# A two-branch attention kernel: shared PSUM banks, paired queries, adding DMAs and a shift pass on GpSimd

## The chip, the cores and the metric

The kernel runs on one core of one Trainium2 chip. The metric is the device time of one execution, in microseconds. The engines are named as in the profile: PE (TensorE, matmuls), DVE (VectorE), ACT (ScalarE), POOL (GpSimd), SP (SyncE, which issues the DMAs here). PSUM, where the PE writes, has eight banks of 128 x 512 fp32.

## The reference

x has 2048 rows of 512. Branch A is full attention with 32 heads of 16; branch B is attention over eight earlier rows at distances 0, 2, ... 14 of the same x, with its own weights. A gate per row mixes them.

```
scores = einsum("bhqd,bhkd->bhqk", q, k) * (Dh ** -0.5)      # A: 32 heads, 2048 x 2048
o = einsum("bhqk,bhkd->bhqd", softmax(scores), v);  a = o @ A_wo
logits = einsum("bhsd,bhswd->bhsw", q, kg) * scale            # B: kg, vg = k, v at s - 2w, w = 0..7
o = einsum("bhsw,bhswd->bhsd", softmax(where(mask, logits, -1e9)), vg);  b = o @ B_wo
g = sigmoid((x * gate_w).sum(-1));  out = g * a + (1 - g) * b
```

## The kernel before, in words

**Branch A.** The queries are cut into four blocks of 512 (QW) and the heads into eight groups of four (NG). A *period* is one block and one group: 32 periods. In a period each of 16 key tiles of 128 meets four heads: 64 score blocks of 128 keys x 512 queries. The PE makes them (`qk`) in *sets* of three and two blocks, which go to two rings of PSUM banks (rA three, rB two). ACT turns a set into exp(scores), the bf16 tile pT (`ex`), three buffers a ring. The PE multiplies pT by V with a column of ones, so that acc, one bank, holds numerator and denominator of four heads (`pv_run`, `pv_mm`). At the end of a period DVE transposes acc to accT (`po1`), inverts the denominators (`po2`), POOL multiplies by the gate and the inverse (`po2a`, `po2b`), DVE transposes into oat (`po3`), and after eight periods the output products follow.

**339 blocks beside ACT.** `n_dve` (line 20) gives 3 to 12 blocks a period, 339 of 2048 in all, to DVE (`d_set`). The PE writes such a score into the bank D (`dq`), and DVE makes from it, with one multiply and add in integers, a number whose bits are roughly those of the exponential (`p1`, into a dt buffer). Three blocks make a group. For each group three shift passes (`sh`) add a constant to the 1536 integers, into pd buffers, and the PE adds all NV = 4 versions into acc with V weighted by WEIGHTS (vd_all), which smooths the error of the rough exponential.

**Queries.** `q_proj` makes Q for one period: 16 matmuls with 32 columns each, because four heads have to lie on rows 32 j and each is stored twice, plain and as absolute value (wq2). DVE copies the result out (`ev`, 0.68 us) and masks the sign bits of the second half (`ab`).

**Branch B.** For each of 16 row tiles (`b_tile`) the PE makes k, v and q; k and v go to DRAM (kv_scr), and SP loads them back shifted, in two halves of four distances (ksh, vsh, 512 KB each). POOL does nearly all the arithmetic in pieces of 128 x 256: products, tree of additions, softmax, the products with v (`av_mul`) and 14 additions of them (`av_add`), into obb. The PE transposes obb (`fin`) for the output products.

**PSUM.** rA 3, rB 2, misc 1, acc 1, D 1. misc is the one bank of all projections of both branches, their evictions and the zero matmuls that keep the PE busy.

**The order.** All work is written down as operations with an engine, planned duration, due time (`dl`), what they depend on, and buffers that they take and use (`Op`, `tok`). `list_schedule` (line 159) plays them out with these durations, each engine taking the candidate that is due first among those that can start soon. The order that comes out is the program's: each engine works its own list in that order, and waits in place if something is late. `avail` asks when a buffer of a resource comes free, `start` gives a due time its bonuses, GFIRST puts POOL's short steps ahead, URG raises work that holds misc. A buffer resource is a count (`Res`), and its buffers go round in turn.

Of the kernel before, what the change touches and what calls it, by code (L numbers as in the profile page):

```python
# [9 lines left out]
ALU = mybir.AluOpType  # L10
# [10 lines left out]
    dve_tiles=3,  # L21
# [15 lines left out]
DEXP = 56  # L37
NV = 4
NGR = 3
NPD = 3  # L40
# [4 lines left out]
NDE = 2  # L45
NDL = 4
SPREAD = (0.75, 0.8)
STEP = 32.0
WEIGHTS = (0.240234375, 0.2021484375, 0.169921875, 0.142578125)
# [10 lines left out]

class Tok:
    def __init__(self, res):
        self.res, self.ops = res, []


class Op:

    def __init__(self, eng, occ, fn, dl, deps=(), alloc=(), use=(), lat=None, rel=0.0, name="",
                 mode="f", js=(), full=0.0, fill=False, scores=None, after=(), ride=False, parts=None):
        self.scores, self.ride, self.parts = scores, ride, parts  # L70
# [17 lines left out]
GFIRST = -300.0  # L88
PRE = 0.14
GP = lambda kind, n: [(False, PRE), (True, NS[kind] * n)]  # L90
# [11 lines left out]
P1D, SHD, LASTD, PO1D = -100.0, 2.0, 200.0, 300.0  # L102
# [56 lines left out]
def list_schedule(ops, zeros):  # L159
# [15 lines left out]

    def avail(o):
        t = o.ready
        for tk in o.alloc:
            r = tk.res
            n = len(r.order)  # L180
            if n >= r.cap:
                for u in r.order[n - r.cap].ops:
                    if u.done is None:
                        return INF
                    t = max(t, u.end + SELF[u.eng] if u.eng == o.eng else u.done)
        return t

    arr = Array()

    def start(e, o):  # L190
        t = avail(o)
        if t == INF:
            return t, 0.0
        if e != "pe":
            return max(free[e], t), o.dl
        t0, end, _, _ = arr.plan(o, t)
        rides = o.mode == "r" and arr.mode == "r" and end < arr.end + 0.05
        return t0, o.dl + ((ALONE if o.ride else KEEP) if o.mode != arr.mode else 0.0) - (RIDE if rides else 0.0)
# [3 lines left out]
    while len(out) < len(ops):  # L202
# [24 lines left out]
        if e == "pe":  # L227
            tz, n = arr.idle(o, t)
            if n > 0:
                z = zeros(n)  # L230
                tz = max([tz, avail(z)] + [u.t for tk in z.alloc[0].res.order[-2:] for u in tk.ops if u.done is not None and u.t < t])
                if tz + n * PASS + (0.0 if o.mode == "c" else SWITCH) <= t + 0.05:
                    for tk in z.alloc:
                        tk.res.order.append(tk)
# [3 lines left out]
        for tk in o.alloc:  # L238
            tk.res.order.append(tk)
# [16 lines left out]
        out.append(o)  # L256
        for s_ in succ.get(o, ()):
            left[s_] -= 1
            if left[s_] == 0:
                s_.ready = max([s_.rel] + [d.end + SELF[d.eng] if d.eng == s_.eng else d.done for d in s_.deps] + [d.t for d in s_.after])  # L260
                cand[s_.eng].append(s_)
# [4 lines left out]
def kernel(  # L266
# [29 lines left out]

    def misc_ps(shape, dtype=FP32, tag="misc"):
        return ps.tile(shape, dtype, tag=tag, bufs=1, name="misc_ps")
# [50 lines left out]
    def op(eng, occ, fn, dl, **kw):  # L349
        if any(tk.res is res.get("misc") for tk in kw.get("use", ())):  # L350
            dl -= URG[eng]
# [6 lines left out]
    def tok(tag, cap):  # L358
        if tag not in res:
            res[tag] = Res(cap)  # L360
        return Tok(res[tag])
# [30 lines left out]
    for pi, (own, groups) in enumerate(seq):  # L392
        n = sum(len(g) for g in groups)
        left = [(gi, u_) for gi, g in enumerate(groups) for u_ in g]
        total, taken = len(own), 0
        for t, j in own:
# [4 lines left out]
            if left and n - len(left) < n * taken / (SPREAD[n // 10] * total) and all(u_[0] == pi for u_ in cur):  # L401
                js = [u_[2] for u_ in cur]
                pick = [x for x in left if x[0] == left[0][0] and x[1][1] not in js]
                if not pick and n - len(left) + 1 < n * taken / (SPREAD[n // 10] * total):
# [12 lines left out]
    wq2 = const.tile([128, DC, H, 2, DH], BF16, name="wq2")  # L417
# [6 lines left out]
    NH = NG // 2  # L424
    woarr = const.tile([128, NH, D], BF16, name="woarr")
    ident = const.tile([128, 128], BF16, name="ident")
    identf = const.tile([128, 128], FP32, name="identf")
    rowc = const.tile([128, 3], FP32, name="rowc")
    wts = const.tile([128, NV], BF16, name="wts")
# [7 lines left out]
    vd_all = const.tile([128, NV, NTD, H, DH + 1], BF16, name="vd_all")  # L437
# [5 lines left out]
    pd_a = const.tile([128, NPD * NGR * ROW], BF16, name="pd_a")  # L443
# [3 lines left out]
    pd_bufs = [pd_a[:, k_ * NGR * ROW:(k_ + 1) * NGR * ROW].rearrange("p (q n) -> p q n", q=NGR) for k_ in range(NPD)]  # L447
    stage = [pd_a[:, k_ * DC * D:(k_ + 1) * DC * D].rearrange("p (c n) -> p c n", c=DC) for k_ in range(2)]
    ott2 = const.tile([128, 2, BPC, 32], BF16, name="ott2")
# [3 lines left out]
    e1 = const.tile([128, NT], FP32, name="e1")  # L453
    d1 = const.tile([128, NT], FP32, name="d1")

    def init_dve():
# [9 lines left out]
        for m in range(NV):  # L466
            V.memset(wts[:, m:m + 1], WEIGHTS[m] * 2.0 ** -DEXP)

# [10 lines left out]
    def init_pool2():  # L479
        make_identity(nc, identf[:])  # L480
# [19 lines left out]
    def load_x(sc):  # L500
        def s():
            xl = work.tile([128, W // 2, D], BF16, name="xld", tag="gat", bufs=NGA) if sc < NGA else stage[1]
# [4 lines left out]
    wst = {}  # L507

    def load_w(part):
        def s():  # L510
            if part == 0:
                wst["q"] = stage[0]
                out = wst["q"]
            else:
                out = wkv[:, :, (part - 1) * D:part * D]
# [18 lines left out]
    tw = tok("pd", NPD)  # L534
# [7 lines left out]
    o_wq = op("sp", 0.5, load_w(0), -8.5, lat=12.5, alloc=[tw])  # L542
# [13 lines left out]
    def q2(E, i):  # L556
        def s():
            a0 = wst["q"][:, :, 4 * i * DH:4 * (i + 1) * DH]
# [6 lines left out]
    o_q2 = [op("dve", 0.5, q2(V, 0), 0.0, deps=[o_wq], use=[tw])]  # L565
    o_q2 += [op("pool", 1.5, q2(G, i), 4.0 + i, deps=[o_wq, o_k3[1]], use=[tw]) for i in range(1, NG)]
# [5 lines left out]
    o_warm = op("pe", 4.0, warm, -9.0, deps=[o_init_d], alloc=[tok("misc", 1)])  # L572
# [34 lines left out]
    def k_proj(i, sc, tag, dl, rel=0.0):  # L607
        st = {}
        tk = tok(tag, 1)
# [16 lines left out]
    def k_bound(i, dl):  # L626
        st = {}
        tk = tok("acc" if i == 0 else "misc", 1)
# [741 lines left out]
```

## Time and profile before

| | us |
|---|---|
| median of 3 runs | 826.01 (825.94 to 826.19) |
| profiled execution, time | 826.04 |
| profiled execution, span of the core | 824.3 |
| first pT starts | 19.67 |
| last pT ends | 815.49 |
| last POOL piece of branch B ends | 796.50 |

The span runs from the first to the last instruction; granted clock 0.994. A group of the profile is a set of instructions with the same tiles: their number, busy time together, mean duration in ns, and the idle time of the engine before them with what ended it. Nearly all instructions are recorded at a helper's line (L323, L332), so tiles tell them apart: pT<-ring is the exponential, acc<-pT the product with V, misc_ps<-bw a projection of branch B, dt_a<-D and wkv<-D the rough exponential (wkv serves as dt buffers once the K and V weights are used up), pd_a<-dt_a and pd_a<-wkv a shift pass. Rows that the steps use:

| row | count | mean ns |
|---|---|---|
| DVE shift pass pd_a<-dt_a, pd_a<-wkv | 195 + 144 | 941, 945 |
| DVE rough exponential | 195 + 144 | 680, 682 |
| DVE eviction of Q, mask | 32, 32 | 684, 538 |
| POOL products prod<-vsh,lg | 256 | 652 |
| POOL additions ob<-prod, ob<-ob,prod, obb<-ob,prod | 32, 64, 32 | 726, 729, 732 |
| POOL copies wq (256 bf16), wk (448 bf16) | 14, 2 | 400, 562 |
| PE Q projections misc_ps<-xT,wq | 512 | 382 (overlapping) |

SP's DMAs: ksh and vsh 512 KB in 3.9 and 3.7 us from issue to landing, kvs 256 KB in 2.0, out 128 KB in 1.7.

### The profile page before, as it was taken

The numbers are of one execution on the slowest core, as the hardware profiler recorded it, in microseconds if no ns is written. First come the engines' busy times: TensorE is split into PE (matmuls) and PEld (weight loads), VectorE is DVE, ScalarE is ACT, GpSimd is POOL, SyncE is SP. The second block draws the span as 40 slices with busy tenths as digits, with TensorE's granted clock in tenths as the row PEclk, the third lists the DMA queues.
The fourth block names the chain that finished last, engine by engine and source line by source line (L and its number), as shares of the span: only waits on it lengthen the run. The fifth ranks groups of instructions, "written<-read, shape, count | busy, mean of one in ns | idle before, by whom it ended". The sixth has DMA issues, their size and how long they took to land.

```text
span 824.3 us, 18657 instructions
## 1 busy us (share of the span) xinstructions
PE 777.9 (94%) x7314; PEld 247.4 (30%) x7358; DVE 706.3 (86%) x1111; ACT 785.9 (95%) x706; POOL 720.4 (87%) x1196
## 2 busy tenths in 40 slices
PE   7999999999999999999999999999999999999996
PEld 4333433333322222222222222222222222222231
DVE  5456876788978999989999899999989899998987
ACT  3899999999899899999999999999999999999995
POOL 5097999999999999899999999899999999899960
PEclk9899999999999999999999999999999999999999
DMA  9203020112111220211112111211111211110000
GB/s 296 78 3 116 2 90 28 65 52 65 57 48 65 65 66 28 63 53 47 63 35 77 57 50 51 65 53 49 43 52 54 82 34 65 52 52 27 27 1 26
DMA packets 44440, 47.37 MB, mean 57 GB/s; under 512 B 2352, under 2 KB 41776, under 8 KB 44352
## 3 DMA queue, kind: packets, MB, share of 16 engines
q1 hardware_dynamic: 44352, 46.18, 17.6%
q8 instruction: 57, 0.93, 0.5%
q14 instruction: 31, 0.25, 0.1%
HBM read 39.85 MB, written 6.32 MB: 56 GB/s over the span
## 4 chain that ended last, share of the span: by engine, by line
ACT 47%; PE 31%; issue 18%; DVE 2%; DMA 1%; SPq 0%; DVEq 0%; ACTq 0%
ACT pT L323 46%; PE acc L332 11%; PE ring L332 9%; PE misc_ps L332 8%; PE D L332 3%; DMA xld<-in_A_x_dram 1%; ACT lg L323 1%; DVE pd_a L323 0%; DVE kt_all L323 0%; PE pxt L584 0%; PE misc_ps L1011 0%; DVE dt_a L323 0%; DVE qt L323 0%; DVE vp_all L323 0%; DVE wkv L323 0%
## 5 line engine op out<-in xcount | busy, mean ns | idle before, releaser
L323 ACT ACTIVATE pT<-ring 128x1536 bf16<-128x1536 f32 (+1 forms) x684 | 778.8, 1319 | 20.5 <-PE acc L332 14.0
L332 PE MATMUL ring<-qt,kt_all 32*128 32x512 bf16 x1709 | 272.0, 382 | 28.4 <-ACT pT L323 19.2
L323 POOL TENSOR_TENSOR prod<-prod 128x256 f32<-128x256 f32 x352 | 235.6, 677 | 13.2
L332 PE MATMUL acc<-pT,vp_all 128*17 128x512 bf16 (+1 forms) x1709 | 189.0, 385 | 0.3 <-DVE accT L323 0.2
L323 POOL TENSOR_TENSOR prod<-ksh,qb 128x256 f32<-128x256 bf16 x256 | 166.5, 673 | 22.5 <-DMA ksh<-kv_scr 21.7
L323 DVE TENSOR_SCALAR pd_a<-dt_a 128x1536 uint16<-128x1536 uint16 x195 | 180.4, 941 | 1.2
L332 PEld LDWEIGHTS <-kt_all 32*128 32x128 bf16 x2048 | 91.2, 91 | 294.1 <-issue 285.2
L323 DVE TENSOR_SCALAR dt_a<-D 128x512 uint16<-128x512 f32 x195 | 132.7, 680 | 39.2 <-PE D L332 38.5
L323 POOL TENSOR_TENSOR prod<-vsh,lg 128x256 f32<-128x256 bf16 x256 | 162.0, 652 | 0.0
L323 DVE TENSOR_SCALAR pd_a<-wkv 128x1536 uint16<-128x1536 uint16 x144 | 131.0, 945 | 1.9 <-PE acc L332 0.3
L332 PE MATMUL acc<-pd_a,vd_all 128*17 128x512 bf16 x1017 | 130.0, 381 | 0.0
L332 PE MATMUL D<-qt,kt_all 32*128 32x512 bf16 x339 | 128.7, 380 | 1.0 <-DVE kt_all L323 0.4
L323 DVE TENSOR_SCALAR wkv<-D 128x512 uint16<-128x512 f32 x144 | 98.2, 682 | 7.5 <-PE D L332 5.9
L332 PE MATMUL misc_ps<-z 128*32 128x512 bf16 x260 | 85.3, 387 | 1.6 <-DVE z L323 1.6
L332 PEld LDWEIGHTS <-vp_all 128*17 128x17 bf16 (+1 forms) x1709 | 43.7, 88 | 74.9 <-issue 66.6
L332 PEld LDWEIGHTS <-vd_all 128*17 128x17 bf16 x1356 | 42.3, 88 | 64.3 <-issue 51.5
L332 PE MATMUL misc_ps<-bw,xT 128*128 128x512 bf16 x162 | 51.6, 393 | 2.4 <-DVE kt_all L323 0.8
L323 POOL TENSOR_TENSOR ob<-ob,prod 128x256 f32<-128x256 f32 x64 | 45.5, 729 | 0.0
L332 PEld LDWEIGHTS <-z 128*32 128x32 bf16 x341 | 29.9, 96 | 42.2 <-issue 26.1
L332 PEld LDWEIGHTS <-xT 128*128 128x128 bf16 x576 | 30.2, 98 | 36.8 <-issue 31.8
L332 PE MATMUL misc_ps<-xT,wq 128*32 128x512 bf16 x512 | 40.5, 382 | 0.1
L323 DVE TENSOR_SCALAR_CACHE_REDUCE kt_all<-misc_ps,rowc 128x512 bf16<-128x512 f32 x32 | 23.8, 746 | 16.0 <-PE misc_ps L332 15.4
(85 smaller groups left out, 611.9 us busy)
## 6 DMA issues: line engine op xcount, KB each, us to landing
ksh<-kv_scr SPq DMA_DIRECT2D x32, 512.0 KB, 3.9
vsh<-kv_scr SPq DMA_DIRECT2D x32, 512.0 KB, 3.7
kv_scr<-kvs SPq DMA_DIRECT2D x16, 256.0 KB, 2.0
out_dram<-osb SPq DMA_DIRECT2D x16, 128.0 KB, 1.7
xld<-in_A_x_dram SPq DMA_DIRECT2D x3, 512.0 KB, 6.4
bw<-in_B_wqkv_dram SPq DMA_DIRECT2D x1, 1536.0 KB, 11.5
wkv<-in_A_wqkv_dram SPq DMA_DIRECT2D x2, 512.0 KB, 7.3
pd_a<-in_A_x_dram SPq DMA_DIRECT2D x1, 512.0 KB, 8.4
```

The costliest lines, as they stand in the source:

```text
L323: return chain_on(key, f(*a, **k))
L332: return chain(nc.tensor.matmul(out, lhsT=lhsT, rhs=rhs, start=start, stop=stop, **kw))
```

## The change

It has seven parts, made together.

1. **Three shared banks.** misc, acc and D are replaced by three banks that any of them may take; which one is settled by the list, at each taking. At most two acc are open at once (`acc_two`).
2. **Queries by eight heads.** Periods 0 and 1 keep `q_proj`. From then on one product of 128 columns makes Q of two periods (`q_pair`); DVE copies it out once and masks it once, and SP writes both to DRAM (q_scr) and reads them back in the layout of each period: two writes and two reads a pair. qt has four buffers, not three.
3. **Adding DMAs.** The products with v of the first half go to av (four slots), those of the second half to prod; POOL issues a DMA that adds prod to av in place, twice, and a third that adds two slots of av to the other two. One addition in two pieces remains. The last two tiles keep additions on POOL. prod has three buffers.
4. **A list with margins.** What another engine awaits from POOL is planned 3 to 4 us later than it should be there (MARGIN). Products with V get a bonus when ACT is four sets ahead (PVU, PVN).
5. **One shift pass a period on POOL**, the third pass of a period's first group (POOL_G), with a buffer of its own.
6. The unshifted version of the rough exponential uses V itself, the others use weights relative to it (DEXP, WEIGHTS, three copies in vd_all, of four tiles now). `dq` waits for the dt buffer and for vd_all, where `p1` did.
7. Buffers: dt one early and three late, for two and four; accT, ott2, oat, obt one each, for two. The rough exponentials of a period are spread over 0.88 of it, for 0.8 (0.6 in the last). Output products are due earlier.

n_dve is as before: 339 blocks.

```diff
-    dve_tiles=3,
+    dve_tiles=4,
-DEXP = 56
+DEXP = -2.0565
-NDE = 2
-NDL = 4
-SPREAD = (0.75, 0.8)
+NDE = 1
+NDL = 3
+SPREAD = (0.75, 0.88, 0.6)
-WEIGHTS = (0.240234375, 0.2021484375, 0.169921875, 0.142578125)
+WEIGHTS = (0.83984375, 0.70703125, 0.59375)
+DMAQ, DMAL = 1.0, 6.0
+NPR = 3
+POOL_G, NPG = (0,), 1
+MARGIN = {("pool", "pe"): 4.0, ("pool", "dve"): 3.0, ("pool", "act"): 3.0, ("pool", "sp"): 3.0, ("dve", "pool"): 1.5}
+QD = 20.0
+PVU, PVN = 100.0, 4
...
+    def known(d, o):
+        if d.eng == o.eng and not d.far:
+            return d.end + SELF[d.eng]
+        return d.done + MARGIN.get((d.eng, o.eng), 0.0)
...
+            t = max(t, min(freed(o, b, 1) for b in r.banks) if isinstance(r, Banks) else freed(o, r.order, r.cap))
...
+        urge = PVU if o.of is not None and last[0] - o.of >= PVN else 0.0
...
     def misc_ps(shape, dtype=FP32, tag="misc"):
+        if tag in ("misc", "acc"):
+            bank, = [tk.bank for tk in now[0].alloc if isinstance(tk.res, Banks)]
+            tag = f"m{bank}"
         return ps.tile(shape, dtype, tag=tag, bufs=1, name="misc_ps")
...
+        name = "banks" if tag in ("misc", "acc") else tag
+            res[name] = Banks(3) if name == "banks" else Res(cap)
...
+    def q_pair(pi, dl, rel):
...
+                    mm(st["p"][:], wq[:, c, 4 * i * DH:4 * (i + 2) * DH], xT[:, c, c_ * QW:(c_ + 1) * QW], c == 0, c == DC - 1)
...
+        w = [op("sp", 0.5, put(0), dl - 5.0, deps=[c], use=[tqs], lat=2.2), op("sp", 0.5, put(1), dl - 4.0, deps=[b], use=[tqa], lat=2.2)]
+        for e in range(2):
+            q_tok[pi + e] = tok("qt", 4)
+            o_q[pi + e] = op("sp", 0.5, get(e), dl - 1.0 + e, deps=w, alloc=[q_tok[pi + e]], lat=2.2)
+    for pi in range(2, NP, 2):
+        q_pair(pi, S0[pi] - QD, S0[pi - 2] - 2.0)
...
+        def av_sum(wp):
+            def s():
+                if wp is None:
+                    G.dma_start(out=av[:, 0:WP, :], in_=av[:, WP:WH, :], accum_op=ALU.add)
+                else:
+                    G.dma_start(out=av[:, wp:wp + WP, :], in_=st["av", wp][:], accum_op=ALU.add)
+            return s
...
+            if t < NT - 2:
+                return op("pool", DMAQ, av_sum(wp), tb + 41, deps=deps, use=use, lat=DMAQ + DMAL, far=True, name=f"B{t}")
...
-        tx = tok("D", 1)
+        tx = tok("misc", 2)
...
+        deps = [o_q[pi], o_k[i][t // TPC], o_vd[(4 * i + j, t)]]
+        a = op("pe", 0.0, dq, tn - 3.0, mode="r", js=[j], deps=deps, alloc=[tx] + ([g["td"]] if first else []),
...
+            if on_pool(m):
+                pb = pd_bufs[NPD + d_count[3] % NPG]
+                a = op("pool", 0.0, sh(m, pb), GFIRST, deps=list(g["p1"]), alloc=[tp], use=[g["td"]], name=f"sg{pi}",
+                       after=d_sg[-1:], parts=GP("one", NGR * QW))
...
-        dl = E + (4.0 + 4.0 * tt if last else 10.0 + 14.0 * tt)
+        dl = E + (4.0 + 4.0 * tt if last else 2.0 + 4.0 * tt)
```

## The prediction

> **What bounds the kernel now.** First the engine totals and the 40 slices of the page: ScalarE (ACT) is busy 95%, and no slice between the start and the end is under 8 tenths.
>
> ```profile
> PE 777.9 (94%) x7314; PEld 247.4 (30%) x7358; DVE 706.3 (86%) x1111; ACT 785.9 (95%) x706; POOL 720.4 (87%) x1196
> DVE  5456876788978999989999899999989899998987
> ACT  3899999999899899999999999999999999999995
> POOL 5097999999999999899999999899999999899960
> ```
>
> So the 684 activations that turn scores into pT set the time, and the change leaves their number alone (1709 blocks on ACT, 339 beside it). It can win only time in which ACT stands or starts late. The second view is the ACT groups, shapes apart; its last columns are idle time and what ended it:
>
> ```profile
> L323 ACT ACTIVATE pT<-ring 128x1536 bf16<-128x1536 f32 x342 | 523.1, 1530 | 14.5 <-PE acc L332 8.2 <-PE ring L332 5.7 <-PE D L332 0.3
> L323 ACT ACTIVATE pT<-ring 128x1024 bf16<-128x1024 f32 x341 | 378.2, 1109 | 6.0 <-PE acc L332 5.8
> ```
>
> Idle before pT is 20.5 us. 5.2 of it precedes the first pT (19.67 us); 15.3 remain, 14.0 ended by a matmul into acc: the PE, which works in a fixed order, came late to the product that frees a pT buffer. The third view, busy time per 40 us, says when (columns: span, PE, PEld, DVE, ACT, POOL, clock, DMA share, GB/s):
>
> ```profile
> 20.00:60.00 40.00, 36.45 (x459) 14.72 (x462) 21.50 (x40) 36.39 (x34) 19.60 (x32) 0.91 0.15 43
> 60.00:100.00 40.00, 37.96 (x439) 15.05 (x440) 29.11 (x56) 38.28 (x36) 34.31 (x57) 1.00 0.18 60
> ...
> 180.00:220.00 40.00, 37.88 (x390) 14.93 (x392) 34.59 (x57) 36.06 (x34) 37.83 (x58) 1.00 0.16 48
> ...
> 260.00:300.00 40.00, 38.06 (x316) 11.04 (x320) 37.00 (x56) 37.84 (x36) 37.74 (x65) 1.00 0.21 64
> ...
> 500.00:540.00 40.00, 38.16 (x335) 10.57 (x335) 37.02 (x56) 40.00 (x38) 37.07 (x64) 1.00 0.15 48
> ```
>
> ACT lacks 3.6 + 1.7 + 3.9 + 2.2 us in these four early windows, with 0.7 at 140:180 it is **12.1 us before 300 us**, and some 3.2 after. The fourth view shows why early: the tile views of misc_ps (one bank for all projections) and of D (one bank for the 339 scores of VectorE) end in their busy share by slice:
>
> ```profile
> busy tenths in 40 slices 9999999999977756547756954764756767553874
> ```
>
> ```profile
> busy tenths in 40 slices 0111222234334655455555555555554555556442
> ```
>
> The first line is misc_ps: full for 230 us, while K, V and Q are still made. The second is D: mostly empty then. Work that may not use the empty bank queues in the full one. In the timeline at 204.6 us ACT stands 1.90 us while VectorE holds an eviction behind a 0.94 us shift pass and PE stands behind that.
>
> There is lateness that no idle row shows, because successive activations overlap. Six in a row took 6.88 us and two 2.44, so a pair adds (6.88 - 2.44)/2 = 2.22; 342 pairs need 759.5 us, the 16 softmax exponentials at most 8.0. From 19.7 to 815.5 us there are 795.8: 28.3 us are lost, 15.3 as idle and 13.0 hidden. This is all the change can get. The tail after the last pT is 8.8 us, and the execution took 826.04 us against a span of 824.3 (1.74 around it); the median of the runs is 826.01, so the two are one scale.
>
> **The change part by part.**
>
> *Three shared banks.* misc, acc and D become one pool of three; two acc may be open at once. Nothing is added. Slice by slice the old demand is 1.0 + 1.0 + 0.1 to 0.4 banks early and about 0.6 + 1.0 + 0.5 late, so 2.1 to 2.4 of three: the queue in misc gets the share of D that stood empty. I take three quarters of the 12.1 us: **-9.1**. Below: all of it. Above: 0, if the order and not the bank keeps PE late (rival 1). The transposes of acc waited 3.3 us for PE, and PE 0.2 for them, so the second acc is worth little by itself.
>
> *Queries by eight heads.* Fifteen pairs replace 30 periods of sixteen 32-column matmuls (16 in 1.05 us in the timeline) by four full ones each (four in 1.03): PE 30 x 1.05 - 15 x 1.03 = -16 us, about 0.5 us a period. VectorE loses 15 evictions (684 ns) and 15 masks (538): -18.3. Twelve of the 14 Pool copies of wq go: -4.2 at the start, while Pool waits for data anyway. Added: four DMAs a pair on SP's queue, through DRAM. Nearest rows: 256 KB from kvs landed in 2.0 us, 128 KB out in 1.7; a write and a read are some 4 us, against a due time about 20 us ahead of the period. They stand on SP behind waits for Pool ("SPq <- POOL prod" 421.9 us, longest 12.9), so they could be 13 us late and still land. Cost: 0; without that cover a period's start would wait out the excess.
>
> *Adding DMAs.* In 14 of 16 tiles 12 of 14 additions leave Pool: 14 x 12 x 0.73 = -122.9 us. Three DMA issues a tile come: 42. No row shows one from Pool. Below 0 (an issue is not busy time), above 1.4 (the eight woarr issues held SP 11.0 us); I take 1.0, as two ksh issues of the same 512 KB held SP 1.91. So +42. The third addition and the last add wait for a landing: the nearest row is ksh, 512 KB in 3.9 us; the same size took 8.7 with every load in flight. Reading the destination too, I take 6, within the 7 that the list plans (DMAQ + DMAL: a constant of the order, not a measurement). The next tile's products stand between.
>
> *A shift pass on Pool.* 32 of 339 VectorE passes go: 32 x 0.943 = -30.2. No row shows 1536 uint16 elements on Pool. Below: copies of 256 and 448 bf16 took 400 and 562 ns, 0.84 ns an element more, so 1.5 us. Above: the two-input product, 256 in 652 ns, six times: 3.9. I take 1.7, nearer the one-input row: +54. PE waits for this pass where it waited for VectorE; behind the product stand the scores of the next sets, and so ACT. Cover: the list places it 4 us late (MARGIN). If Pool is later, each us past that reaches ACT.
>
> *Sums.* VectorE 706.3 - 30.2 - 18.3 = 658, in late windows 37.0 becomes about 34.6 of 40: an eviction finds it free sooner. Of the late 3.2 us I take half, **-1.6**, and of the hidden 13.0 a sixth, **-2.2**. Pool 720.4 - 122.9 + 42 + 54 - 4.2 = 689, some 2 us less a tile (46.6 to 44.6). One early dt buffer for two, three late for four: groups of three scores come some 5 us apart and hold a buffer about 12, so three suffice; early groups wait in the list and no engine does. wts and the vd products keep their size (3 x 4 tiles for 4 x 3): 0. accT, ott2, oat and obt go from two buffers to one: in exchange the output products of a block are due 2 + 4 us a tile after its last head, not 10 + 14, so the next block's first transposes, some 50 us later, find them free: 0, and up to 0.7 us of VectorE's wait four times if not. Margins: 0 by themselves, the price is order. The start (x, K, first Q) and the tail chain (transpose, product, 0.68 us eviction, DMA) stay: 0.
>
> Together -9.1 - 1.6 - 2.2 = -12.9: 826.0 - 12.9 = **813**.
>
> **The rivals.**
>
> *1. The banks were not the reason.* ACT's idle ends at PE's order, and VectorE's rows before the evictions stay early on (21 to 35 of 40 busy, not full). For it: the 339 scores now compete for the same banks and now also wait on PE, not VectorE, for their dt buffer. Against: the full misc line. Then 12.1 us stay and only the others come, less what the new waits give back: **825**. Chance 0.10, mostly within 0.2%.
>
> *2. Pool stands for the landings* (slower). An addition that depends on a landing stops Pool in order, and with it the shift passes, softmax sums and SP's loads. Pool saves 2.0 us in each of 14 tiles, and its last piece ended at 796.5, 28 us ahead of the end: 56 us of room. Two waits a tile, 28, each landing time over 7 us: room is gone from 7 + 56/28 = **9.0 us**. At 10 us: 28 x 3 - 56 = +28, with the 13 us won, **841**. For it: Pool is at 9 tenths throughout, 8.7 us has been seen for this size; against: that was the start's crowd, while DMA is 11 to 20% busy later, and ksh took 3.9. Chance 0.20.
>
> *3. Pool's issues are held up by VectorE.* The uint32 mask on VectorE, 256 elements, takes 0.35 us at 17.64 and 0.87 at 210.75 beside Pool's products, so the two engines do block each other. If an issue had to wait out the shift passes (three in a row took 2.67 us), 42 x 2.67 = 112 of Pool's room of 56 are used: +56 - 13, **869**; if only for the third of the time that those passes run and half of one row of them, 42 x 0.35 x 1.3 = 19, nothing. Chance 0.06 for a loss. (The Trainium skill, SBUF — State Buffer, section "SBUF: two separate sides", box "DVE blocks DMA", says just this of DMAs issued from GpSimd: descriptors cannot be written while VectorE runs in a two-port mode. It speaks against this part of the change; no run here shows such a DMA yet.)
>
> **How the numbers follow.** Forecast 0.64 (faster), rival 1 0.10 (0.07 same, 0.03 slower), rival 2 0.20, rival 3 0.06 (both slower). 0.2%, about 1.7 us, is what a measurement can tell from no change. Faster 0.64, same 0.07, slower 0.29. Low end: three quarters of all 28.3 us lost, 826 - 21 = 805; I put 804. High end: rival 2 at 10 us, 841. Beyond lie the worse landings and rival 3. The forecast's own range is 804 to 822.
>
> **What would show it.** Right: ACT's four early windows at 39 or more of 40, "ACT pT <- PE acc" under 6 us, VectorE near 658 busy, pT still 684. Wrong by rival 1: those windows unchanged. By rival 2: POOL waits for a DMA of av, prod or obb, in tens of us, landings over 9 us, Pool ending later than 796.5. By rival 3: long gaps on Pool at its DMA issues. A shift pass on Pool over 3 us, or PE waiting for Pool's pd_a, would break the margin step; a late qt the query step.

## The result, and the profile after

| | before | after |
|---|---|---|
| median of 4 runs each, same chip | 826.1 (825.94 to 826.51) | 857.38 (856.79 to 858.52) |
| span of the profiled execution | 824.3 | 856.2 |
| first pT starts | 19.67 | 19.5 |
| last pT ends | 815.49 | 847.6 |
| last POOL piece of branch B ends | 796.50 | 831.3 |
| last POOL instruction ends (after: a shift pass) | 796.50 | 835.4 |

The ratio is 1.038, with a 95% interval of 1.0362 to 1.0398: the kernel became slower by 31 us, where 13 us faster was forecast, and the time lies outside the range of 804 to 841. The same views as before, first the engine totals and slices on the page of the changed kernel:

```profile
PE 764.1 (89%) x6964; PEld 244.9 (29%) x7019; DVE 675.5 (79%) x1048; ACT 791.1 (92%) x706; POOL 764.9 (89%) x1090
...
DVE  5546776889667898989887998877778899778787
ACT  3999999988999898999998999989899999899995
POOL 3398999999999999999999999999999959999990
```

VectorE lost work, 706.3 to 675.5 (658 was forecast), and so did the PE. POOL rose from 720.4 to 764.9, where 689 was forecast, and stands at nine tenths nearly until the end. ACT has eights in slices that were meant to be filled. The chain that ended last, by engine and then by group, says the same more sharply (in the kernel before, its engine line began with ACT 47%, and POOL was not in it):

```profile
POOL 69%; PE 9%; DMA 7%; ACT 6%; issue 5%; DVE 4%; SPq 0%; DVEq 0%; POOLq 0%; ACTq 0%
POOL prod L364 36%; POOL pd_a L364 12%; POOL av L364 12%; PE misc_ps L373 6%; ACT pT L364 6%; DMA av<-prod 5%; POOL lg L364 4%; PE ring L373 2%; POOL obb L364 2%; POOL ott L364 2%; DMA ksh<-kv_scr 1%; DVE pd_a L364 1%; DMA xld<-in_A_x_dram 1%; POOL rden L364 1%; DMA kv_scr<-kvs 0%
```

The end is now set by POOL. Why POOL has more work than reckoned stands in its groups, shapes apart (count, busy time, mean ns, idle before):

```profile
L364 POOL TENSOR_SCALAR pd_a<-wkv 128x1536 uint16<-128x1536 uint16 x16 | 66.8, 4173 | 0.0
L364 POOL TENSOR_SCALAR pd_a<-dt_a 128x1536 uint16<-128x1536 uint16 x16 | 66.2, 4140 | 24.6 <-DVE dt_a L364 24.5
...
L364 POOL DMA_DIRECT2D av<-prod x28 | 24.9, 888 | 8.1 <-POOL prod L364 8.1
```

A shift pass takes POOL 4.1 to 4.2 us, not 1.7; the 32 of them take 133 us, not 54. (VectorE does the same pass in 0.94.) An adding DMA costs POOL 0.89 us to issue, where 1.0 was estimated. The two groups of adding DMAs landed 6.2 us after issue (av<-prod) and 4.9 (av<-av), against 6 taken.

What this does to the other engines: the waits of the changed kernel (total us, number, longest),

```profile
PE misc_ps L373 <- POOL pd_a L364: 30.3, 22, 3.0
ACT pT L364 <- PE ring L373: 29.8, 26, 5.1
...
POOL pd_a L364 <- DVE dt_a L364: 24.5, 2, 21.6
ACT pT L364 <- PE misc_ps L373: 16.1, 18, 3.1
```

and one such wait in the timeline (start, length, engine; in brackets the idle time before and who ended it):

```profile
306.07 4.34 POOL L364 TENSOR_SCALAR pd_a<-wkv 128x1536 uint16<-128x1536 uint16 x1
...
310.46 0.39 PE L373 MATMUL misc_ps<-pd_a,vd_all 128*17 128x512 bf16 x3 [1.26 <-POOL pd_a L364]
...
311.75 0.39 PE L373 MATMUL ring<-qt,kt_all 32*128 32x512 bf16 x3
...
312.25 4.62 ACT L364 ACTIVATE pT<-ring 128x1536 bf16<-128x1536 f32 x4 [1.23 <-PE ring L373]
```

The list had planned the pass at 1.83 us. POOL ends it at 310.41; the PE stood 1.26 us for it, the scores of the next set follow at 311.75 in its fixed order, and ACT, which eats those scores, stood 1.23 us. Where it happens is seen in the busy time per 40 us (columns: stretch, its length, PE, PEld, DVE, ACT, POOL, clock, DMA share, GB/s):

```profile
20.00:60.00 40.00, 37.33 (x477) 14.41 (x482) 20.39 (x40) 39.72 (x36) 24.38 (x35) 1.00 0.26 74
...
180.00:220.00 40.00, 36.07 (x340) 13.39 (x340) 34.66 (x50) 35.94 (x33) 38.70 (x56) 1.00 0.38 98
...
300.00:340.00 40.00, 33.39 (x285) 9.77 (x288) 34.93 (x54) 36.06 (x33) 38.24 (x53) 0.96 0.40 100
500.00:540.00 40.00, 36.16 (x318) 10.59 (x318) 34.30 (x51) 38.30 (x35) 39.05 (x56) 1.00 0.32 84
```

Before POOL has a queue (20 to 60 us) ACT lacks only 0.3 us, where it lacked 3.6: the forecast's gain is there. From 140 us to 820 us POOL is busy 37.5 to 39.6 of 40 in all stretches but two, and ACT lacks up to 4.1 of 40.

### The profile page after: what moved, and what is told of

It is laid out like the page before. It is cut to its first block, busy times and chain, and to the rows that moved or that the text cites. A ratio compares the mean times of both kernels' runs of the same rounds, so it can differ in the third digit from the quotient of the medians.

```text
span 856.2 us, 17997 instructions
## 1 busy us (share of the span) xinstructions
PE 764.1 (89%) x6964; PEld 244.9 (29%) x7019; DVE 675.5 (79%) x1048; ACT 791.1 (92%) x706; POOL 764.9 (89%) x1090
## 3 DMA queue, kind: packets, MB, share of 16 engines
q1 hardware_dynamic: 52752, 54.05, 20.3%
## 4 chain that ended last, share of the span: by engine, by line
POOL 69%; PE 9%; DMA 7%; ACT 6%; issue 5%; DVE 4%; SPq 0%; DVEq 0%; POOLq 0%; ACTq 0%
POOL prod L364 36%; POOL pd_a L364 12%; POOL av L364 12%; PE misc_ps L373 6%; ACT pT L364 6%; DMA av<-prod 5%; POOL lg L364 4%; PE ring L373 2%; POOL obb L364 2%; POOL ott L364 2%; DMA ksh<-kv_scr 1%; DVE pd_a L364 1%; DMA xld<-in_A_x_dram 1%; POOL rden L364 1%; DMA kv_scr<-kvs 0%
## 5 line engine op out<-in xcount | busy, mean ns | idle before, releaser
L373 PE MATMUL misc_ps<-pT,vp_all 128*17 128x512 bf16 (+1 forms) x1709 | 205.1, 388 | 0.7 <-DVE accT L364 0.4
L364 POOL TENSOR_TENSOR prod<-prod 128x256 f32<-128x256 f32 (+1 forms) x256 | 167.9, 670 | 5.9
L364 DVE TENSOR_SCALAR wkv<-misc_ps 128x512 uint16<-128x512 f32 x192 | 129.3, 683 | 48.1 <-PE misc_ps L373 39.9
L373 PE MATMUL misc_ps<-pd_a,vd_all 128*17 128x512 bf16 x1017 | 132.1, 386 | 33.9 <-POOL pd_a L364 30.3
L373 PE MATMUL misc_ps<-qt,kt_all 32*128 32x512 bf16 x339 | 127.1, 385 | 4.2 <-DVE wkv L364 1.5
L364 DVE TENSOR_SCALAR dt_a<-misc_ps 128x512 uint16<-128x512 f32 x147 | 98.8, 684 | 39.5 <-PE misc_ps L373 31.0
L364 POOL TENSOR_SCALAR pd_a<-dt_a 128x1536 uint16<-128x1536 uint16 x16 | 66.2, 4140 | 24.6 <-DVE dt_a L364 24.5
L364 POOL TENSOR_TENSOR prod<-vsh,lg 128x256 f32<-128x256 bf16 x128 | 82.3, 736 | 0.0
L364 POOL TENSOR_TENSOR av<-vsh,lg 128x256 f32<-128x256 bf16 x128 | 78.4, 646 | 0.0
L364 POOL TENSOR_SCALAR pd_a<-wkv 128x1536 uint16<-128x1536 uint16 x16 | 66.8, 4173 | 0.0
```

The source lines that it names most:

```text
L364: return chain_on(key, f(*a, **k))
L373: return chain(nc.tensor.matmul(out, lhsT=lhsT, rhs=rhs, start=start, stop=stop, **kw))
```

## The experiments

Theory P: the change is a gain of about 10 us, and POOL's shift pass, 4.1 us long and 32 times, takes it away and more. Two rivals inside it: the *length* fills POOL (throughput), or the *wrong plan* of 1.83 us makes the order bad. Rivals outside it: the adding DMAs hold POOL up (the prediction's rivals 2 and 3), or banks and queries lost what they were to win.

### 1. Without the pass

The 32 passes go back to VectorE; the rest of the change stays.

```diff
-POOL_G, NPG = (0,), 1
+POOL_G, NPG = (), 1
```

> The changed kernel with all shift passes on VectorE again. Theory P: GpSimd became the bound, because 32 shift passes took 4.16 us each there (133 us, where 54 were reckoned). Without them POOL is busy 765 - 133 = 632 us, ACT carries the chain again, VectorE gets 32 x 0.94 = 30 us back (about 705): 812 to 822 us. Rival O: another part (shared banks, paired queries, adding DMAs or the margins) costs the time: still over 835 us. Rival M: both share it: 823 to 835.

Measured: 816.09 (815.39 to 817.36), ratio to the kernel before 0.9882 (0.9867 to 0.9897). Faster than both. Its engine totals and chain:

```profile
PE 752.3 (92%) x6962; PEld 246.3 (30%) x7018; DVE 690.1 (85%) x1080; ACT 785.6 (97%) x706; POOL 633.8 (78%) x1058
...
ACT 47%; PE 27%; issue 18%; POOL 4%; DVE 3%; DMA 1%; SPq 0%; DVEq 0%; ACTq 0%
```

POOL has fallen to 78% and is nearly out of the chain, which again is ACT's. VectorE has its 32 passes back, 29 us in its rows, but its busy time grew by 14.6 us only, to 690.1 and not to the 705 that was expected: with the pass on POOL some of its other work had been recorded longer (the mask qa<-qs 758 ns in the mean, 471 here; the scaling of kt_all 1780 and 1310). That is also a part of why the changed kernel's VectorE is not at the 658 of the forecast. The groups of pT and the early stretches of this kernel:

```profile
L364 ACT ACTIVATE pT<-ring 128x1536 bf16<-128x1536 f32 x342 | 522.6, 1528 | 10.4 <-PE ring L373 9.8
L364 ACT ACTIVATE pT<-ring 128x1024 bf16<-128x1024 f32 x341 | 378.0, 1109 | 0.0
```

```profile
60.00:100.00 40.00, 37.71 (x420) 14.17 (x420) 27.11 (x50) 39.13 (x36) 35.80 (x59) 1.00 0.18 61
...
180.00:220.00 40.00, 37.99 (x371) 13.99 (x375) 31.05 (x50) 39.83 (x37) 36.87 (x60) 1.00 0.41 100
260.00:300.00 40.00, 38.59 (x325) 11.45 (x328) 38.76 (x59) 39.56 (x36) 38.53 (x66) 1.00 0.41 103
```

Of ACT's idle time 5.1 us stand before the first pT, so 5.3 us are left of 15.3. Before 300 us it lacks 4.9 us in all, where it lacked 12.1. The pass alone therefore costs 857.4 - 816.1 = 41 us here, and theory P stands. The granted clock was 0.983 in the changed kernel's profile and 0.994 here. A score matmul took 387 and 382 ns, and the PE makes 9% of the changed kernel's chain: by estimate that is 1 us of the 41. POOL's wait for the landing of av<-prod is 35.0 us in this kernel, more than in the changed one (8.4), and costs little: POOL is 4% of the chain.

### 2. The pass planned at its true length

```diff
-                       after=d_sg[-1:], parts=GP("one", NGR * QW))
+                       after=d_sg[-1:], parts=[(False, 4.12)])
```

> The changed kernel; only the planned duration of GpSimd's shift pass is 4.12 us instead of 1.83, so the order knows the true price. Theory P (throughput of GpSimd): its work stays at 765 us, so 840 to 860 us, though PE's 30 us of waiting for pd_a should shrink under 15. Rival V: only the order was misled by the wrong duration: 826 us or less.

Measured: 862.91 (860.35 to 866.65), ratio 1.0451 (1.0413 to 1.0488), 3 us over the 840 to 860 that were expected. The view of pd_a lists no wait of PE for POOL's pass any more, where it was 30.3 us, and yet the kernel is no faster. In 40 slices:

```profile
ACT  3999989999999669999999999999999999999950
POOL 3398997999899989889899999999999999999995
```

ACT finished its last pT at 826.4, 32 us ahead of the end, and then there is nothing for it to do; POOL worked on to 849.1. So it is POOL's throughput: a better order moves the waiting from the middle to the end. (The chain of this run's page names ACT with 47% and POOL with 4%. Followed back from the end, it runs on POOL from 848.4 to 811.3 us and leaves it there over a wait of 0.86 us for VectorE, so its shares say little of how full POOL is before.) (The sixes near 290 us are one stall of 14.6 us, which comes back below.)

### 3. The pass as 32-bit additions

Two 16-bit integers lie in one 32-bit word and no carry passes between them, so 768 integer additions of a constant with both halves filled do the pass of 1536. The constant is a second operand, read again and again.

```diff
+                if on_pool(m):
+                    o_, i_ = pb.bitcast(I32)[:, :, 0:QW // 2], g["dt"].bitcast(I32).rearrange("p (q n) -> p q n", q=NGR)
+                    G.tensor_tensor(out=o_, in0=i_, in1=_ap(step2[:], [list(step2[:].ap[0]), [0, NGR], [0, QW // 2]]), op=ALU.add)
+                    return
...
-                       after=d_sg[-1:], parts=GP("one", NGR * QW))
+                       after=d_sg[-1:], parts=GP("ff", NGR * QW // 2))
```

> The changed kernel; GpSimd's shift pass adds to two 16-bit numbers at once, as 768 32-bit integers with a broadcast constant (a two-input addition) instead of 1536 16-bit integers with a scalar, planned at 1.77 us. Theory P: by the additions of 256 fp32 in 0.735 us the pass takes 1.8 to 2.0 us, POOL is busy 765 - 72 = 693 us, and the time is 812 to 825. Rival O: over 835. If a 32-bit pass takes 4 us too, the cost isn't that of the 16-bit form and the time stays near 857.

Measured: 829.07 (828.03 to 830.46), ratio 1.0038 (1.0023 to 1.0053). Its POOL groups:

```profile
L365 POOL TENSOR_TENSOR pd_a<-dt_a,step 128x768 int32<-128x768 int32 x16 | 23.5, 1471 | 28.8 <-DVE dt_a L365 28.6
L365 POOL TENSOR_TENSOR pd_a<-wkv,step 128x768 int32<-128x768 int32 x16 | 23.5, 1467 | 12.3 <-DVE wkv L365 12.2
```

The pass now costs what the prediction had given it (1.47 us, with 1.7 taken), POOL is busy 680.9 us (with 689 forecast), and 28 of the 41 us are won back. The other 13 are not: the time is 4 us over the range that was expected. ACT shows two long stalls, 6.1 us from 287.6 and 4.2 us from 334.2; the granted clock was 0.70 from 290 to 300 us and 0.64 from 340 to 350. The second stall ends a chain of DMAs: the write of a query pair took 5.36 us from 329.99 on, its read began at 335.49, and the scores waited for it.

### 4. The pass alone, in the kernel before

The third pass of each period's first group goes to POOL in the old kernel, in the rotation of its pd buffers and with the short plan (1.83); nothing else changes.

```diff
-                V.tensor_scalar(out=o_, in0=i_, scalar1=STEP * m, scalar2=None, op0=ALU.add)
+                (G if m == NV - 1 and gi == 0 else V).tensor_scalar(out=o_, in0=i_, scalar1=STEP * m, scalar2=None, op0=ALU.add)
```

> The kernel before, with only this part of the change: the third shift pass of a period's first group on GpSimd, planned at 1.83 us, in the rotation of the same three pd buffers. Theory P: POOL's 720 us grow by 133 to 853; with some 49 us before its first product and 28 after its last that is about 930 us (900 to 935). Rival V (GpSimd's time is covered, only the order suffers): under 850.

Measured: 945.51 (945.14 to 946.65), ratio 1.1445 (1.1426 to 1.1465), 10 us over the range that was expected. POOL is busy 852.0 us, and 720.4 + 32 x 4.1 = 852. The engine line of the chain:

```profile
POOL 59%; PE 23%; DVE 8%; ACT 5%; issue 4%; DMA 1%; SPq 0%; POOLq 0%; ACTq 0%; DVEq 0%
```

The pass costs 119 us in a kernel whose POOL has only some 28 us of room, and 41 in one whose POOL had been relieved by adding DMAs. The cause is the same, the price is not. The 119 us hold more than POOL's time: the pass stands in VectorE's rotation of pd buffers here, and the granted clock was 0.921, where it was 0.994 before; what each of these is worth was not tried.

### 5. Without adding DMAs, without the pass

From here to experiment 9 the basis is the kernel of experiment 1, and one part is undone in each. Here all 14 additions of a tile are POOL's again.

```diff
-            if t < NT - 2:
+            if False:
```

> All shift passes on VectorE, and the additions back on GpSimd in place of the adding DMAs. POOL is busy 634 + 14 x (12 x 0.73 - 3 x 0.89) = 719 us, as in the kernel before. Theory: with no long pass on it, GpSimd still keeps up (796 us end in the kernel before), ACT stays the chain, the adding DMAs are worth little: 815 to 820 us against 816.1 with them. Rival: the relief of GpSimd is what made that kernel faster: 822 or more.

Measured: 817.31 (817.17 to 817.49), ratio 0.9899 (0.9883 to 0.9916); against 816.09, about 1 us, which is within the spread of experiment 1 (815.39 to 817.36). POOL is busy 712.1 instead of 633.8. With ACT setting the end, 78 us of POOL's time are worth next to nothing: without the pass the adding DMAs are hardly needed. What they are worth in the changed kernel, with the pass, was not tried by itself; experiment 4 suggests that it is much.

### 6. Three fixed banks

misc, acc and D have one bank each again, and dq takes D.

```diff
-        if tag in ("misc", "acc"):
-            bank, = [tk.bank for tk in now[0].alloc if isinstance(tk.res, Banks)]
-            tag = f"m{bank}"
+        if tag in ("misc", "acc", "D"):
+            tag = f"m{tag}"
...
-        tx = tok("misc", 2)
+        tx = tok("D", 1)
```

> All shift passes on VectorE, and misc, acc and D one bank each again instead of three shared ones. Theory of the prediction: the shared banks are worth 9 us of early idle time of ACT: 821 to 827 us, with ACT's idle time before 300 us back over 8 us. Rival 1 of the prediction: the banks weren't the reason; 815 to 819.

Measured: 843.06 (842.39 to 844.13), ratio 1.0211 (1.0196 to 1.0227). 27 us slower than experiment 1, and 16 over the range that was expected. Up to 300 us ACT lacks 20.3 us, where it lacked 4.9; that is 15 of the 27. One stall of 8.5 us at 273.5 is in it, and two of 4.8 and 4.7 us come at 664 and 811. Of the parts that are undone one at a time here, after the pass itself, this is the one whose loss is largest. The size is that of this order: the kernel before, with fixed banks and its own order, lacked 12.1 us there. Shared banks alone in the kernel before were not tried.

### 7. Queries period by period

q_proj for all 32 periods, with wq2 for all heads and three qt buffers.

```diff
-    for pi in range(2, NP, 2):
-        q_pair(pi, S0[pi] - QD, S0[pi - 2] - 2.0)
+    for pi in range(2, NP):
+        q_proj(pi, "misc", S0[pi] - 10.0, rel=S0[pi - 1] - 6.0)
```

> All shift passes on VectorE, and every period's queries made alone again (16 matmuls of 32 columns, own eviction and mask, no DMAs through DRAM). VectorE has 18 us more, PE 16 us more. Theory: this costs 1 to 4 us (817 to 820), since VectorE and PE have room. Rival: queries carry most of the gain: 822 or more. Rival: their DMAs cost: under 815.

Measured: 829.0 (827.79 to 830.62), ratio 1.0041 (1.0026 to 1.0056): 13 us slower than experiment 1. VectorE is busy 710.4 instead of 690.1 (+20.3; the prediction had counted 18.3), the PE 765.9 instead of 752.3 (+13.6; 16 counted). Idle time ahead of pT is 24.4 us instead of 10.4. The time is 9 us over the range that was expected, so the rival "queries carry most of the gain" came. But the losses do not add up: 27 us for the banks and 13 for the queries are more than the 10 us that all parts without the pass win together, so each is the price of taking one part out of an order made for all, and not its share of the gain. Of the 13 us, ACT lacks 4.8 and 3.5 us in the two stretches from 700 to 780 us, with a granted clock of 0.91 in both.

### 8. Without margins

```diff
-MARGIN = {("pool", "pe"): 4.0, ("pool", "dve"): 3.0, ("pool", "act"): 3.0, ("pool", "sp"): 3.0, ("dve", "pool"): 1.5}
+MARGIN = {}
```

> All shift passes on VectorE, and no margins in the list (MARGIN empty). Theory: PE, VectorE and ACT then stand for GpSimd's results now and then: 817 to 825 us, with waits for POOL rows over 10 us. Rival: without a pass on GpSimd nothing urgent comes from it, so the margins do nothing: 815 to 817.

Measured: 816.8 (814.42 to 821.07), ratio 0.9898 (0.9865 to 0.993). No difference from experiment 1 that the spread lets through: where the PE no longer waits for POOL, a margin for POOL does nothing that could be measured.

### 9. More blocks beside ACT

```diff
-    n_dve=(3, 3, 6, 6, 6, 9, 9, 9) + (12,) * 24,
+    n_dve=(3, 3, 6, 9, 9, 9, 9, 9) + (12,) * 20 + (15,) * 4,
```

> All shift passes on VectorE, and 357 blocks beside ACT in place of 339 (9 in periods 3 and 4, 15 in the last four). ACT loses 18 x 0.447 = 8.0 us of work, VectorE gains 18 x 0.68 + 18 x 0.94 = 29 us (690 to 719). Theory: ACT is the chain again, VectorE has the room that the queries left: 806 to 812 us. Rival: VectorE is late for the evictions then: 816 or more.

Measured: 835.5 (835.07 to 838.31), ratio 1.0126 (1.0106 to 1.0146). Missed by over 20 us. ACT's work fell by 6.8 us to 778.8 (8.0 were reckoned), but a stall of 7.2 us came at 194.8, and after the last pT, at 810.1, 23.7 us still stood, with rough exponentials and their products in them, where experiment 1 has 8.9. ACT is not the bound in the last period once VectorE has 15 blocks in it.

### 10. The pair addition, planned at 1.45 us and queries 10 us earlier

Experiment 3 left 13 us. First theory: wrong plan and late queries. The edit is shown against the kernel of experiment 3.

```diff
-QD = 20.0
+QD = 30.0
...
-                       after=d_sg[-1:], parts=GP("ff", NGR * QW // 2))
+                       after=d_sg[-1:], parts=[(False, 1.45)])
```

> The 32-bit pass on GpSimd once more (1.47 us measured), now planned at 1.45 in place of 1.77, and the pair queries due 30 us ahead in place of 20. Theory: what kept the 32-bit pass at 829 us were two stalls of ACT, 6.4 us at 287 (one of the order) and 4.2 us at 334 (a qt that came late through DRAM); with another list they go or move: 814 to 823 us, and no wait for qt. Rival: a pass on GpSimd costs as such, through PE's waits: 826 or more.

Measured: 827.27 (822.17 to 831.37, 10 runs), ratio 1.001 (0.9985 to 1.0035), over the 814 to 823 that were expected. The wait for a query is gone, and the time hardly moves. The longest stall that is left stands in the timeline:

```profile
298.33 0.72 DVE L365 STREAM_TRANSPOSE accT<-misc_ps 128x512 f32<-128x512 f32 x1
...
299.11 0.71 PE L374 MATMUL misc_ps<-pT,vp_all 128*32 128x512 bf16 x4
...
299.93 2.59 ACT L365 ACTIVATE pT<-ring 128x1536 bf16<-128x1536 f32 x2 [7.32 <-PE misc_ps L374]
```

ACT stood 7.32 us, because all its pT buffers waited for the first product of a new period (128*32), which got its acc bank only after the old acc was transposed; meanwhile the banks went to scores for VectorE. It is not the only loss. The timeline and the stretch of 10 us (columns as before) show another:

```profile
208.25 3.07 DVE L365 TENSOR_SCALAR qa<-qs 128x256 uint32<-128x256 uint32 x1
208.27 2.84 POOL L365 TENSOR_TENSOR prod<-ksh,qb 128x256 f32<-128x256 bf16 x4
...
211.96 0.62 PE L374 MATMUL misc_ps<-bw,xT 128*128 128x512 bf16 x2 [1.60 <-DVE kvs L365]
```

```profile
210.00:220.00 10.00, 7.62 (x42) 1.36 (x37) 5.79 (x8) 6.75 (x7) 9.68 (x17) 0.62 0.81 190
```

The mask of the queries, 0.28 us at its shortest in this run, took 3.07 us while POOL ran four products; the eviction kvs came behind it, the PE stood 1.60 us for that, and the granted clock then fell to 0.62 in the mean of these 10 us (0.50 from 213 to 222), in which ACT lacks 3.3 us. The granted clock also goes with the spread of the ten runs: 822.17 and 822.76 us at 0.993, 831.27 and 831.37 at 0.978. Experiment 1 ran at 0.993 to 0.995, so at the same clock the two kernels are some 6 us apart, not 11. Whether the clock falls because the PE stands, or both have another cause, is not settled by these runs.

### 11. The pass by itself

Behind the work of experiment 1's kernel stand, three times over, five POOL instructions on data that nobody reads, so the outputs are unchanged: the scalar addition over six pieces with gaps (the kernel's form) and over 1536 elements in one piece, in uint16; the same on bf16; on 768 fp32; and a copy of 1536 uint16.

```diff
+    for _ in range(3):
+        G.tensor_scalar(out=a16, in0=l6, scalar1=STEP, scalar2=None, op0=ALU.add)
+        G.tensor_scalar(out=pd_a[:, 0:NGR * QW].bitcast(U16), in0=l16, scalar1=STEP, scalar2=None, op0=ALU.add)
+        G.tensor_scalar(out=pd_a[:, 0:NGR * QW], in0=dt_bufs[0], scalar1=STEP, scalar2=None, op0=ALU.add)
+        G.tensor_scalar(out=pd_a[:, 0:NGR * QW].bitcast(FP32), in0=dt_bufs[0].bitcast(FP32), scalar1=STEP, scalar2=None, op0=ALU.add)
+        G.tensor_copy(out=pd_a[:, 0:NGR * QW].bitcast(U16), in_=l16)
```

> Behind the kernel's own work (all shift passes on VectorE) stand three rounds of five GpSimd instructions on 128 x 1536 16-bit numbers, with nothing beside them: the shift pass as it is (6 runs of 256 in, 3 of 512 out), the same with plain runs of 1536, as bf16, as 768 fp32, and a copy of 1536 uint16. They change no output; the time grows by some 40 us and isn't compared. Theory K (the scalar addition on 16-bit integers is slow by itself): 4.09 us for the first two, under 2 for the copy. Rival S (the shape): the plain runs take under 2. Rival C (VectorE beside it held it up): the first takes under 2 here.

Its time as a whole (860.78 once) was not compared with anything. Its POOL groups from 780 us on:

```profile
L365 POOL TENSOR_SCALAR pd_a<-dt_a 128x1536 uint16<-128x1536 uint16 x6 | 24.4, 4085 | 29.7 <-DVE pd_a L365 16.2 <-DVE rden L365 13.5
L365 POOL TENSOR_SCALAR pd_a<-dt_a 128x1536 bf16<-128x1536 bf16 x3 | 12.3, 4085 | 0.2
L365 POOL TENSOR_SCALAR pd_a<-dt_a 128x768 f32<-128x768 f32 x3 | 6.4, 2129 | 0.2
L365 POOL COPY pd_a<-dt_a 128x1536 uint16<-128x1536 uint16 x3 | 4.4, 1464 | 0.2
```

The other engines end at 818.2 us, so the last two rounds have nothing beside them: 4085 ns, in either layout and 16-bit type; half the elements, as fp32, take 2129. A line through these two lengths has (4085 - 2129) / 768 = 2.55 ns an element and 0.17 us fixed (an estimate: the shorter length was measured in fp32 only). A copy of the same 1536 takes 1464 ns. So it is neither contention with VectorE, nor the gaps, nor the 16-bit type: it is the scalar addition on POOL.

### 12. The first product of a period earlier

Theory for the 11 us that experiment 10 still lies behind experiment 1: the stall at the change of period. In the kernel of experiment 10 the first product of each period is now due 200 us earlier, so that it gets its bank ahead of VectorE's scores.

```diff
-        o = op("pe", 0.0, pv, tn + 3.0, mode="c", js=js, full=-(-len(js) // 4), fill=not first,
+        o = op("pe", 0.0, pv, tn + 3.0 - (200.0 if first else 0.0), mode="c", js=js, full=-(-len(js) // 4), fill=not first,
```

> The 32-bit pass on GpSimd as replanned, and in the list the first product of a period with V, which needs a bank for the next acc, comes 200 us earlier in due time. At 292.3 us the replanned kernel's ACT stood 7.3 us: one bank was the old acc, scores for VectorE took the other two as they came free, and the new period's first product waited for a bank until the old acc was transposed at 298.3. Theory: the list gave the scores the banks, and that is most of the 11 us between this kernel and the one without a pass on GpSimd: 814 to 821 us, and no stall of ACT over 3 us. Rival: a pass on GpSimd costs as such: 825 or more.

Measured: 825.51 (822.05 to 827.09, 10 runs), ratio 0.9986 (0.9974 to 0.9999). The stall shrank to 5.6 us only. The two ratios differ by 0.0024, some 2 us, but their intervals overlap, so even that gain is not sure. The theory is not borne out. Why even a pass of 1.47 us on POOL stays 9 us behind none is open. Experiments 2, 3, 10 and 12 all have a stall that begins between 287 and 293 us, which experiment 1 has not. A long stall for a product of pT does not need a pass on POOL, though: the 7.2 us of experiment 9 are one without it, and the 8.5 us of experiment 6 another. That is as far as the runs go.

## Why the prediction was wrong

**The step that failed** is "A shift pass on Pool": "Below: copies of 256 and 448 bf16 took 400 and 562 ns, 0.84 ns an element more, so 1.5 us. Above: the two-input product, 256 in 652 ns, six times: 3.9. I take 1.7, nearer the one-input row: +54." The pass took 4.1 to 4.2 us, above even the upper bound, and 32 of them 133 us. The likeness that was chosen, one input, was not the one that counts: the copy did follow its row (1464 ns in experiment 11, 0.84 ns an element would give 1.5 us), but an addition is not a copy. (The Trainium skill, GPSIMD Engine Reference, section 4.1 "Engine selection", also calls one-input elementwise work on GpSimd "roughly line-rate"; here such a pass took 4.09 us where VectorE took 0.94, and the measurement decides.) The profile before had one row of a scalar operation on POOL, and the prediction did not use it:

```profile
L323 POOL TENSOR_SCALAR rr<-rr,omg 128x32 f32<-128x32 f32 x16 | 5.8, 363 | 7.3 <-DVE rr L323 4.9 <-ACT pT L323 2.1
```

It is a multiplication and far too short to give a price for an element, but its 32 elements took longer than the 64 of a two-input product on POOL (lg<-prod, 308 ns), while a copy of 256 took 400. That was a hint that scalar operations are not priced like copies there.

**POOL's sum** with the measured sizes: 720.4 - 122.9 + 37.5 (28 issues of 0.888 and 14 of 0.900) + 133 - 4.2 = 763.8; 764.9 were measured. 79 us too little on one term made the difference of 764.9 - 689 = 76. The smaller terms are not each as exact as their sum: experiment 5 gives 78 us for additions less issues, where the line reckons 122.9 - 37.5 = 85, and some products are recorded longer. The kernel before ended POOL's part at 796.5; with 43.4 us more that is 839.9, and POOL's last instruction ended at 835.4.

**The room.** The prediction worked out that POOL has 56 us of room if the change saves 2 us a tile. The 79 us go past that. It had even put the sign into a rival, and chose the wrong mechanism for it: rival 2 let POOL run out of room by standing for landings of 9 us and more. Landings were 6.2 and 4.9 us, so that did not happen. Its arithmetic of room, applied to the pass's own upper bound of 3.9 us, would have shown that the gain is gone: 32 x (3.9 - 1.7) = 70 us, 14 past the 56, so 826 + 14 - 13 = 827. The bound was written down, and neither a rival nor the range was made from it.

The arithmetic of room itself was too kind as well. With the measured 79 us it gives 826 + (79 - 56) - 13 = 836, and 857.4 were measured. Half of the 56 was the 28 us between POOL's last instruction and the end. In the changed kernel this gap is still 856.2 - 835.4 = 20.8 us, so only 7 of the 28 were used: the chain stays on POOL until a shift pass that ends at 811.4 us, POOL's last instruction is a shift pass too, and the PE and VectorE still have the rest of the last period to do after it. Work that each period needs cannot move into the room at the end. The 20.8 us that stayed unused are near the 21 that the arithmetic misses; whether they are all of them, the runs do not show.

**The margin step** named its own test ("A shift pass on Pool over 3 us, or PE waiting for Pool's pd_a"), and both came: 4.1 us and 30.3 us of waiting. But the margin was not the point: with the plan corrected the waits went and the time did not get better (experiment 2), and without the pass the margins do nothing that could be measured (experiment 8).

**Rival 1** (banks were not the reason) is not borne out: fixed banks in the new order cost 27 us, 15 of them early (experiment 6). The forecast's three terms, -9.1 early, -1.6 late and -2.2 hidden, can be checked in experiment 1, which is the change without its pass: ACT's early idle time went from 12.1 to 4.9 (-7.2), its late one from 3.2 to 0.4 (-2.8). Hidden lateness: from 19.2 to 804.7 there are 785.5 us, 767.5 are needed, 18.0 lost, 5.3 of them idle, so 12.7 hidden, where it was 13.0 (-0.3). With 0.5 us won at the start the sum is -10.8, and the span fell by 10.7. So the places of the gain were right, mostly early in ACT, and the hidden lateness did not yield. That the early gain is the banks' rests on experiment 6, in the new order alone.

**Rival 3** (issues held up by VectorE) is not seen: 42 issues took 0.82 to 1.06 us each, while VectorE was busy 79%. (The Trainium skill, SBUF — State Buffer, section "SBUF: two separate sides", box "DVE blocks DMA", warns of DMAs issued from GpSimd beside two-port operations of VectorE; no run here shows it, and what kept these free of it was not tried.)

**The queries** were costed at nothing but the busy time they free. Those sizes held within 3 us, but that taking them out costs 13 us was missed (experiment 7): the evictions that went held one of the contested banks each, which is the likely reason and was not tried by itself. The read through DRAM was late once, in experiment 3, by 4.2 us. **The additions**: the issue was right within 0.11 us, the landing within 1.1, and their worth depends on POOL being the bound: 1 us without the pass.

## What to carry to other kernels

Before work goes to an engine that is nearly full, find a row of that very operation on that engine; where there is none, hold the upper bound against the engine's room, and if it is past it, that is a case with a chance of its own, not a number in a range. When an end is set by one engine's throughput, correcting the planned durations or margins only moves the waiting; undoing the one suspect part, alone, separates it from the gain that the others bring (here 41 us lost in a change otherwise worth 10). Relief of an engine that does not set the end is worth next to nothing: without the pass, the adding DMAs freed 78 us of POOL and moved the time by 1.

## What the runs showed of the hardware

- A scalar addition on POOL took 4.09 us for 1536 elements of a partition (bf16, or uint16 in one piece or in six) and 2.13 us for 768 fp32: by a line through the two, an estimate, 0.17 us + 2.55 ns an element. In the changed kernel, beside the other engines, the 1536 took 4.08 to 4.39 us. A copy of 1536 uint16 took 1.46 us, a third.
- An int32 addition of two operands does 768 elements in 1.47 us, 2.8 times less than 1536 16-bit scalar additions for the same result, although it has an input more.
- POOL issues a DMA of 512 KB in 0.89 us; with addition into the destination it lands after 6.2 us (prod to av) and 4.9 (av to av).
- POOL's products prod<-ksh,qb have a mean of 750 ns in the changed kernel and 744 in experiment 1, for 673 before; in the changed kernel those directly behind a DMA issue have a median of 0.95 to 0.97 us. The records overlap, so this may be no cost.
- The uint32 mask of 256 elements on VectorE took 0.28 us at its shortest and up to 3.07 beside POOL's products (experiment 10). Without a pass on POOL it took 0.28 to 0.81 in experiment 1 and up to 2.56 in experiment 8.
- Stretches in which the PE stood were followed by a low granted clock: 0.62 from 210 to 220 us in experiment 10, 0.64 from 340 to 350 in experiment 3.
- The version that was fastest by its median is the changed kernel without the pass: 816.1 us, 1.2% under the kernel before.
